# Where the next unit's first retention job stands: a slot inside the last job of the present unit

## The chip, the cores and the metric

The kernel runs on one core of one Trainium2 chip. The metric is the device time of one execution in microseconds (us). Engines are named as in the profile: PE is TensorE's matmul and PEld its weight load, DVE is VectorE, ACT is ScalarE, POOL is GpSimd, SP is SyncE, which here only issues DMAs.

## The reference

All numbers are float32. Retention in its parallel form runs over 8 batches, 8 heads, 576 positions and 64 dimensions a head; its output, reshaped to 4608 tokens of 512, goes through an RMS norm and a SwiGLU network of width 1536.

```python
# q, k, v: (8, 8, 576, 64)
scores = (1.0 / np.sqrt(D_)) * np.matmul(q, k.transpose(0, 1, 3, 2))
gamma = 1.0 - 2.0 ** (-5.0 - np.arange(H))
rel = pos[:, None] - pos[None, :]
Dmat = np.where(rel >= 0, gamma[:, None, None] ** rel[None, :, :], 0.0)
attn = np.matmul(scores * Dmat[None], v)
x = attn.transpose(0, 2, 1, 3).reshape(B * S, H * D)          # (4608, 512)
xn = x / np.sqrt(np.mean(x * x, axis=-1, keepdims=True) + 1e-06) * rms_g
g = xn @ w_gate
out = (g / (1.0 + np.exp(-g)) * (xn @ w_val)) @ w_out
```

## The kernel before

**Retention jobs.** A job is one batch and one pair of heads; there are 32 (8 batches, 4 pairs), `jobs[j]`. The sequence of a job is cut into nine chunks of 64 positions, so all its matmuls are 64x64 and run on quarters of the PE array, one head of the pair beside the other. A job has these parts:

- `fetch(j)`: SP issues the DMAs of q, k and v (L160, L201, L204).
- `prepare(j)`: DVE transposes q and k (two instructions, L257), ACT scales v by the decay (four, L266).
- `scores(j)` (L285): q times k within each chunk, 40 matmuls in the trace. A float32 matmul stands there as two matmuls with two weight loads.
- `states(j)` (L305): k times v of each chunk, 32 in the trace.
- `weigh(j)`: DVE masks the scores (two instructions, L318) into `ret`.
- `sums(j)`: DVE sums the states up over the chunks with the decay (eight instructions, L332 and L334).
- `values(j)` (L355): masked scores times v into two PSUM banks, 36 in the trace. At its end ACT copies one element into `tick` (`valued`, L364), waiting for the last matmul.
- `carried(j)` (L375): q times the running sums, added into the same banks, 32 in the trace; its first matmul waits for `valued`. Then DVE writes four to six scaled pieces into x (L397).

`slot(j, rest)` puts two jobs together: `values(j - 1)`, `scores(j)`, `states(j)`, `weigh(j)`, `carried(j - 1)`, and then `sums(j)`. Without `rest` it has only job j's parts. `close(j)` is `values(j)` and `carried(j)`.

**Units.** The feed-forward network runs over nine units of 512 tokens. Units 0 and 1, with jobs 0 to 11, stand in a written plan (`PLAN`), which the change doesn't touch. Units 2 to 8 run in the loop at the end of the kernel. A unit has six steps `up(u, n)` for the first two weight matrices and then `across(u)` for the third. Both use a scheme that multiplies two-by-two blocks with seven products instead of eight. `up` is a generator: it gives way seven times, i = 0 to 6, once after each of its seven products; a product is four matmuls of 128x256, eight in the trace (L614), and the names x, y, z, x, w, z, w of the banks are their order. Odd n multiply into `h` on DVE (L621, L633) and take differences (`differences`, L698); even n apply SiLU on ACT (L635).

**What is put between.** The order on every engine is the order in which these calls are made (`tc.manual_schedule`); nothing is moved by a scheduler. In units 2 to 6 (`more`) the retention jobs of one batch stand between the steps of `up`: unit u takes jobs j0 = 4(u + 1) to j0 + 3. After n = 0 comes `slot(j0)` without the rest, after n = 1, 2 and 3 a full `slot(j0 + n)`; `values(j0 + 3)` stands before the last product of n = 4 (i = 5), and `carried(j0 + 3)` after n = 4. These are six stretches of 64x64 matmuls. `prepare(j0 + n)` and `fetch(j0 + n + 1)` stand in n = 1 to 4 at i = 2, so the next unit's first job is prepared in n = 4. In n = 5 ACT squares the four columns of the next unit's x, DVE adds them up (`gather`, L446 and L440), and after i = 4 `root_1` sums them over partitions with one 128x512 matmul (L477).

**Buffers.** PSUM has eight banks, taken in turn by `bank()`: four by a step of `up`, two by `values`, four by `scores` and `states`. q and k transposed and the running sums have two buffers each, `ret` one, v three and k four. Weights come through a ring in SBUF, which `refill` (L580) fills when `used` frees a piece.

Of the kernel before, what the change touches and what calls it, by code (L numbers as in the profile page):

```python
# [41 lines left out]
def kernel(  # L42
# [15 lines left out]
    NHP = H // 2  # L58
# [87 lines left out]
    jobs = [(b, hp) for b in range(B) for hp in range(NHP)]  # L146
# [125 lines left out]
    def side(i):  # L272
        return slice(i * L, i * L + L)
# [3 lines left out]
    def scores(j):  # L277

        d = st[j]
        s = d["s"] = [bank(f"s_{j}_{i}") for i in range(3)]  # L280
        for c in range(NC + 1):
            i, odd = divmod(c, 2)
            c = min(c, NC - 1)
            for e in range(2):
                nc.tensor.matmul(  # L285
                    s[e][side(odd), i * L : i * L + L], lhsT=d["kT"][side(e), c * L : c * L + L],
                    rhs=d["qT"][side(e), c * L : c * L + L], start=True, stop=True,
                )
# [8 lines left out]
    def states(j):  # L297

        d = st[j]
        d["last"] = bank(f"last_{j}")  # L300
        for c in range(NC - 1):
            i, odd = divmod(c, 2)
            o = state_of(d, c)
            for e in range(2):
                nc.tensor.matmul(  # L305
                    o[side(e)], lhsT=d["k"][side(odd), i, e],
                    rhs=d["v"][side(odd), i, e], start=True, stop=True,
                )

    def weigh(j):  # L310

        d = st[j]
        hp = jobs[j][1]
        s = d["s"]
        n = NFULL + 1
        ret = d["ret"] = att.tile([P, 2, n, L], F32, tag="ret", name=f"ret_{j}", bufs=1)
        for e in range(2):
            nc.vector.scalar_tensor_tensor(  # L318
                out=ret[:, e], in0=s[e][:, : n * L].rearrange("p (c k) -> p c k", k=L),
                scalar=float(_gamma(H)[2 * hp + e] ** -L),  # L320
                in1=causal.unsqueeze(1).to_broadcast([P, n, L]), op0=ALU.mult, op1=ALU.mult,
            )

    def sums(j):

        d = st[j]
        hp = jobs[j][1]
        t = d["sum"] = att.tile([P, NC - 1, L], F32, tag="sum", name=f"sum_{j}")
        for c in range(NC - 1):
            part = state_of(d, c)  # L330
            if c == 0:
                nc.vector.tensor_copy(out=t[:, 0], in_=part)  # L332
                continue
            nc.vector.scalar_tensor_tensor(  # L334
                out=t[:, c], in0=t[:, c - 1], scalar=gc[:, hp : hp + 1], in1=part,
                op0=ALU.mult, op1=ALU.add,
            )
        del d["s"], d["last"]

    def follow(a, b):  # L340
        why = mybir.DependencyInfo(mybir.DependencyClass.Sync, mybir.DependencyReason.DATA)
        tc.add_manual_dep(a.ins, b.ins.name, why, reason="rows of the array")

    def column(j, odd, e):

        return side(1 - e if odd and j >= FIRST else e)

    def values(j):

        d = st[j]  # L350
        av = d["av"] = [bank(f"av_{j}_{i}") for i in range(2)]
        for c in range(NC):
            i, odd = divmod(c, 2)
            for e in range(2):
                mm = nc.tensor.matmul(  # L355
                    av[odd][column(j, odd, e), i * L : i * L + L],
                    lhsT=d["v"][side(odd), i, e] if c < NC - 1 else d["vt"][:, e],
                    rhs=d["ret"][side(odd), e, i],
                    start=(c < 2), stop=False, skip_group_check=True,
                )  # L360
        if j < FIRST:
            d["valued"] = nc.gpsimd.memset(tick, 0.0)
        else:
            d["valued"] = nc.scalar.copy(out=tick, in_=mhalf[:1])  # L364
        follow(d["valued"], mm)

    def carried(j):

        d = st[j]
        b, hp = jobs[j]  # L370
        av = d["av"]
        for c in range(1, NC):
            i, odd = divmod(c, 2)
            for e in range(2):
                mm = nc.tensor.matmul(  # L375
                    av[odd][column(j, odd, e), i * L : i * L + L], lhsT=d["sum"][side(e), c - 1],
                    rhs=d["qT"][side(e), c * L : c * L + L],
                    start=False, stop=(c >= NC - 2), skip_group_check=True,
                )
                if c == 1 and e == 0:  # L380
                    follow(mm, d["valued"])
        cut = U // L - b
        for u, c0, c1, o in ((b, 0, cut, b * L), (b + 1, cut, NC, 0)):
            if u not in x_of:
                x_of[u] = xp.tile([P, NHP, U], F32, tag="x", name=f"x_{u}")
            x = x_of[u][:, hp, o : o + (c1 - c0) * L].rearrange("p (c k) -> p c k", k=L)
            for first in (c0, c0 + 1):
                i, odd = divmod(first, 2)
                n = -(-(c1 - first) // 2)
                if n <= 0:  # L390
                    continue
                moves = [(slice(0, P),) * 2]
                if column(j, odd, 0) != side(0):
                    moves = [(side(e), column(j, odd, e)) for e in range(2)]
                for to, at in moves:
                    g = (gq if to == at else gx)[at, hp].unsqueeze(1)
                    nc.vector.tensor_tensor(  # L397
                        out=x[to, first - c0 :: 2],
                        in0=av[odd][at, i * L : (i + n) * L].rearrange("p (c k) -> p c k", k=L),
                        in1=g.to_broadcast([at.stop - at.start, n, L]), op=ALU.mult,  # L400
                    )
        st[j] = {}

    def slot(j, rest=True):

        if rest:
            values(j - 1)
        scores(j)
        states(j)
        weigh(j)  # L410
        if j < FIRST:
            sums(j)
        if rest:
            carried(j - 1)
        if j >= FIRST:
            sums(j)
# [5 lines left out]
    def fetch(j):  # L422
        if j < len(jobs):
            load_qk(j)
            load_kv(j)
# [557 lines left out]
    def store(u, b=None):  # L983

        rows = out[u * U : u * U + U].rearrange("(C c p) (R r x) -> c r p C R x", C=2, c=2, R=2, r=2)
        v4 = vec.rearrange("p (C R) n d -> p C R n d", C=2)
        for n, (r, c) in CORNERS.items():
            if b is None:
                for half in range(2):
                    nc.sync.dma_start(out=rows[c][r][:, half], in_=v4[:, half, :, n])  # L990
            else:
                nc.sync.dma_start(out=rows[c][r][:, b // 2, b % 2], in_=vec[:, b, n])
# [246 lines left out]
    with tc.manual_schedule():  # L1239
        start()  # L1240
        for u in range(2, NU):
            j0 = NHP * (u + 1)
            more = u + 1 < B
            for n in range(2 * NG):
                for i, _ in enumerate(up(u, n)):
                    if n == 1 and i == 4:
                        store(u - 1)
                    if n == 2 * NG - 2 and i == 1:
                        inner_sums(u, 0, 0)
                        inner_sums(u, 1, 0)  # L1250
                    if more and i == 2 and 0 < n <= NHP:
                        if j0 + n < len(jobs):
                            prepare(j0 + n)
                            fetch(j0 + n + 1)
                    if u + 1 < NU and n == 2 * NG - 1:
                        if i < NHP:
                            gather(u + 1, i, square(u + 1, i))
                        elif i == NHP:
                            root_1(u + 1)
                    if more and n == NHP and i == 5:  # L1260
                        values(j0 + NHP - 1)
                if more and n < NHP:
                    slot(j0 + n, rest=(n > 0))
                elif more and n == NHP:
                    carried(j0 + NHP - 1)
            for i, _ in enumerate(across(u)):
                if u + 1 == NU:
                    continue
                if i == 2:
                    root_2(u + 1)  # L1270
                elif i in (3, 4, 5, 6):
                    scale_x(u + 1, (i - 3,))
                elif i == 8:
                    sums_of_x(u + 1)
# [27 lines left out]
```

## Time and profile before

| | us |
|---|---|
| median of 3 runs | 1116.55 (1115.22 to 1117.88) |
| the profiled execution, its own time | 1118.5 |
| its span, first to last instruction | 1116.6 |
| PE busy in the span | 1093.8 |
| DVE busy | 798.5 |
| POOL busy | 467.8 |
| ACT busy | 279.9 |
| 64x64 matmuls of scores, busy (L285) | 28.2 |
| 64x64 matmuls of the carried part, busy (L375) | 27.2 |

The mean granted TensorE clock of the profiled execution was 0.994. A line of the timeline gives the start and the duration in us, the engine, the line of the code, the operation, what it writes and reads, the tile of the array (128\*128 is the whole, 64\*64 a quarter), the size and the number of instructions that are merged into the line. Idle time before it stands in brackets with what ended it; "issue" is time in which the engine waited for nothing that the profile shows. Matmuls are pipelined, so the durations of merged lines overlap, and only starts can be subtracted from each other.

### The profile page before, as it was taken

To read this page: it belongs to the slowest core of one execution; us is meant where nothing else is said; L and a number is where in the kernel's file an instruction comes from. 1 tells how busy PE (TensorE), PEld (TensorE's weight loads), DVE (VectorE), ACT (ScalarE), POOL (GpSimd) and SP (SyncE) were. 2 spreads that over 40 slices of the span, in tenths; PEclk is the share of its full clock that TensorE was granted. 3 is DMA by queue.
4 is the path that set the end of the run, shared out by engine and by line. 5 is a ranking of instruction groups with operands and counts; after the bars stand their busy time and mean duration, and the time that the engine had idled before them with its cause. 6 is when DMAs were issued, how large, how long until landed. Compare 5 with 4: busy or idle time off the path is not lost.

```text
span 1116.6 us, 24381 instructions
## 1 busy us (share of the span) xinstructions
PE 1093.8 (98%) x10102; PEld 915.3 (82%) x10102; DVE 798.5 (72%) x1367; ACT 279.9 (25%) x565; POOL 467.8 (42%) x419
## 2 busy tenths in 40 slices
PE   7899999999999999999999999999999999999998
PEld 6754444469988899889988898889888998898888
DVE  3777768789867786787677786779476945594456
ACT  4556465211121221222022201231122111211110
POOL 0023535557730287025802482229312951393236
PEclk8899999999999999999999999999999999999999
DMA  7765888598678976787769875898485665585471
GB/s 178 205 183 190 285 228 241 211 318 238 221 306 211 207 251 220 212 226 218 281 162 212 284 254 160 242 234 289 150 216 199 238 213 181 165 293 166 158 243 42
DMA packets 253870, 243.72 MB, mean 218 GB/s; under 512 B 193088, under 2 KB 213824, under 8 KB 247616
## 3 DMA queue, kind: packets, MB, share of 16 engines
q1 hardware_dynamic: 252752, 241.87, 70.8%
q8 instruction: 79, 1.29, 0.5%
q10 hardware_dynamic: 1008, 0.30, 0.1%
q14 instruction: 31, 0.25, 0.1%
HBM read 212.05 MB, written 30.08 MB: 217 GB/s over the span
## 4 chain that ended last, share of the span: by engine, by line
PE 90%; DVE 6%; issue 1%; POOL 1%; ACT 1%; DMA 0%; SPq 0%; POOLq 0%; DVEq 0%; ACTq 0%
PE up L674 14%; PE x L614 13%; PE z L614 13%; PE w L614 13%; PE y L614 7%; PE xo L773 6%; PE xp L773 4%; PE zo L773 3%; PE zp L773 3%; PE yo L773 2%; PE av L355 2%; PE wo L773 2%; PE s L285 2%; PE av L375 2%; PE yp L773 1%
## 5 line engine op out<-in xcount | busy, mean ns | idle before, releaser
L674 PE MATMUL up<-x,ring 128*128 128x512 f32 x384 | 166.9, 594 | 1.3 <-DVE x L521 0.8
L614 PE MATMUL x<-x,ring 128*128 128x256 f32 x672 | 161.4, 383 | 0.6 <-DVE t L698 0.6
L738 POOL TENSOR_TENSOR vi<-h 128x384 f32<-128x384 f32 x32 | 38.9, 1217 | 288.6 <-DVE h L633 273.3
L614 PE MATMUL w<-sums,ring 128*128 128x256 f32 x672 | 159.3, 380 | 0.0
L614 PE MATMUL z<-x,ring 128*128 128x256 f32 x672 | 158.7, 379 | 0.0
L674 PEld LDWEIGHTS up<-x,ring 128*128 128x128 f32 x384 | 72.3, 190 | 90.6 <-issue 83.9
L614 PEld LDWEIGHTS z<-x,ring 128*128 128x128 f32 x672 | 127.7, 190 | 19.9 <-issue 2.9
L614 PEld LDWEIGHTS w<-sums,ring 128*128 128x128 f32 x672 | 127.3, 190 | 17.4
L614 PEld LDWEIGHTS x<-x,ring 128*128 128x128 f32 x672 | 125.1, 190 | 18.1 <-DVE t L698 0.7
L743 POOL TENSOR_TENSOR vi<-h 128x384 f32<-128x384 f32 (+2 forms) x46 | 48.0, 1042 | 147.0 <-DVE h L633 147.0
L977 POOL TENSOR_TENSOR vi<-vi 128x512 f32<-128x512 f32 (+2 forms) x63 | 71.9, 1153 | 35.4 <-DVE vi L800 32.6
L640 ACT COPY m<-x 128x512 f32<-128x512 f32 x42 | 24.6, 585 | 229.3 <-PE x L614 229.3
L614 PE MATMUL y<-sums,ring 128*128 128x256 f32 x336 | 79.4, 379 | 0.9 <-DVE sums L533 0.9
L621 DVE TENSOR_TENSOR h<-u,w 128x512 f32<-128x512 f32 x42 | 28.9, 687 | 62.7 <-PE w L614 62.4
L614 PEld LDWEIGHTS y<-sums,ring 128*128 128x128 f32 x336 | 63.8, 190 | 9.9 <-PE x L614 1.3
L621 DVE TENSOR_TENSOR u<-m,y 128x512 f32<-128x512 f32 x42 | 28.8, 685 | 48.1 <-PE y L614 45.4
L635 ACT ACTIVATE h<-h 128x512 f32<-128x512 f32 x63 | 39.6, 630 | 85.3 <-DVE h L621 85.3
L334 DVE SCALAR_TENSOR_TENSOR sum<-sum,gc,s 128x64 f32<-128x64 f32 x192 | 53.9, 281 | 6.8
L1097 POOL TENSOR_TENSOR vi<-vi 128x512 f32<-128x512 f32 (+1 forms) x24 | 40.7, 1698 | 40.7 <-DVE vi L1086 26.8
L743 POOL TENSOR_TENSOR vi<-vi,h 128x384 f32<-128x384 f32 (+2 forms) x46 | 48.9, 1062 | 3.6
L743 POOL TENSOR_TENSOR vi<-h,vi 128x384 f32<-128x384 f32 (+2 forms) x46 | 46.2, 1005 | 3.6
L1097 POOL TENSOR_TENSOR ring<-ring 128x512 f32<-128x512 f32 x24 | 30.4, 1272 | 41.1 <-DVE ring L1086 30.7
(310 smaller groups left out, 2050.1 us busy)
## 6 DMA issues: line engine op xcount, KB each, us to landing
ring<-w_out_blocks SPq DMA_DIRECT2D x59, 1344.0 KB, 6.6
ring<-w_up_blocks SPq DMA_DIRECT2D x42, 1792.0 KB, 8.0
w_out_blocks<-vi SPq DMA_DIRECT2D x21, 448.0 KB, 4.4
out_dram<-vi SPq DMA_DIRECT2D x64, 128.0 KB, 3.1
qraw<-in_q_dram SPq DMA_DIRECT2D x96, 72.0 KB, 5.2
kraw<-in_k_dram SPq DMA_DIRECT2D x96, 72.0 KB, 3.2
k<-in_k_dram SPq DMA_DIRECT2D x48, 128.0 KB, 3.1
v<-in_v_dram SPq DMA_DIRECT2D x48, 128.0 KB, 3.0
```

The costliest lines, as they stand in the source:

```text
L285: nc.tensor.matmul(s[e][side(odd), i * L : i * L + L], lhsT=d["kT"][side(e), c * L : c * L + L], rhs=d["qT"][side(e), c * L : c * L + L], ...
L334: nc.vector.scalar_tensor_tensor(out=t[:, c], in0=t[:, c - 1], scalar=gc[:, hp : hp + 1], in1=part, op0=ALU.mult, op1=ALU.add,)
L614: nc.tensor.matmul(ps[:, i * HU : i * HU + HU], lhsT=w[:, PLACE[blk], c, i * P : i * P + P], rhs=t_of[u][blk][:, c], start=(start and i == ...
L621: nc.vector.tensor_tensor(out=o, in0=a, in1=pairs_of(ps), op=ALU.add)
L635: nc.scalar.activation(out=o, in_=c, func=AF.Silu)
L640: nc.scalar.copy(out=s1, in_=pairs_of(x_))
L674: nc.tensor.matmul(ps, lhsT=w[:, PLACE[blk], c % 2, i * P : i * P + P], rhs=x_of[u][:, c], start=(c == 0), stop=(c == NHP - 1),)
L738: eng.tensor_tensor(out=i1, in0=x12, in1=x11, op=ALU.subtract)
L743: eng.tensor_tensor(out=o[:, c], in0=a[:, c], in1=b[:, c], op=op)
L773: nc.tensor.matmul(ps, lhsT=lhs[:, c], rhs=w[:, s, c], start=((nm, s // 4) not in first), stop=False, skip_group_check=True,)
L977: eng.tensor_tensor(out=t[:, :, o], in0=t[:, :, x], in1=t[:, :, y], op=ALU.add)
L1097: nc.gpsimd.tensor_tensor(out=t[o], in0=t[x], in1=t[y], op=op)
```

## The change

The loop of the units gets another condition. After n = 4, too, a full slot is put: `slot(j0 + 4)`, which is `values(j0 + 3)`, scores and states of the next unit's first job, its `weigh`, `carried(j0 + 3)` and its `sums`. Since that job is then done with its first half, no slot stands after n = 0, except in unit 2, whose first job no unit ahead of it took. In unit 6, where there is no next job, `values` stays before the last product of n = 4 and `carried` after the step. The lines that prepare and fetch stay as they are.

```diff
-                    if more and n == NHP and i == 5:
+                    if more and (n, i) == (NHP, 5) and j0 + NHP == len(jobs):
                         values(j0 + NHP - 1)
-                if more and n < NHP:
-                    slot(j0 + n, rest=(n > 0))
-                elif more and n == NHP:
-                    carried(j0 + NHP - 1)
+                if more and n <= NHP and (n or u == 2):
+                    if j0 + n < len(jobs):
+                        slot(j0 + n, rest=(n > 0))
+                    else:
+                        carried(j0 + n - 1)
```

In the built programs each engine has the same instructions of computation and DMA in both; on PE, DVE and ACT some change places, on POOL and SP none does. PE's program has 44 stretches of 64x64 matmuls before and 36 after, the written plan's among them.

## The prediction

> **What bounds the kernel now.** I read the page first: the busy line and the chain that ended last.
>
> ```profile
> span 1116.6 us, 24381 instructions
> PE 1093.8 (98%) x10102; PEld 915.3 (82%) x10102; DVE 798.5 (72%) x1367; ACT 279.9 (25%) x565; POOL 467.8 (42%) x419
> ...
> q8 instruction: 79, 1.29, 0.5%
> ...
> PE 90%; DVE 6%; issue 1%; POOL 1%; ACT 1%; DMA 0%; SPq 0%; POOLq 0%; DVEq 0%; ACTq 0%
> ```
>
> TensorE (PE) is busy for 98% of the span and carries 90% of the chain. From 300 us on, the PE timeline has only four marked pauses (0.91, 1.17, 0.61 and 0.72 us). So in the units the change touches, the end moves by what PE's own queue gains or loses. DVE, ACT, POOL and SP count only if they make PE wait.
>
> "Busy" hides what the change is about, so next I read the PE timeline of unit 5 by start times, not by durations (ends are modelled). A step of one `product` is eight 128x256 matmuls, and start to start it takes 1.727 us. Here are the first stretch (after n=0), the full slot after n=3, and the two pieces of n=4:
>
> ```profile
> 677.28 1.89 PE L614 MATMUL w<-sums,ring 128*128 128x256 f32 x8
> 679.10 0.81 PE L285 MATMUL s<-qT,kT 64*64 64x64 f32 x40
> ...
> 680.31 1.99 PE L614 MATMUL x<-x,ring 128*128 128x256 f32 x8
> 682.14 1.89 PE L614 MATMUL y<-sums,ring 128*128 128x256 f32 x8
> ...
> 719.87 1.89 PE L614 MATMUL w<-sums,ring 128*128 128x256 f32 x8
> 721.69 0.69 PE L355 MATMUL av<-ret,v 64*64 64x64 f32 x32
> ...
> 723.37 0.67 PE L375 MATMUL av<-qT,sum 64*64 64x64 f32 x32
> 723.97 1.99 PE L614 MATMUL x<-x,ring 128*128 128x256 f32 x8
> 725.80 1.89 PE L614 MATMUL y<-sums,ring 128*128 128x256 f32 x8
> ...
> 732.71 1.89 PE L614 MATMUL z<-x,ring 128*128 128x256 f32 x8
> 734.53 0.69 PE L355 MATMUL av<-ret,v 64*64 64x64 f32 x32
> 735.04 0.28 PE L355 MATMUL av<-ret,vt 64*64 64x64 f32 x4
> 735.26 1.99 PE L614 MATMUL w<-sums,ring 128*128 128x256 f32 x8
> 737.18 0.69 PE L375 MATMUL av<-qT,sum 64*64 64x64 f32 x32
> 737.81 1.99 PE L614 MATMUL x<-x,ring 128*128 128x256 f32 x8
> 739.64 1.89 PE L614 MATMUL y<-sums,ring 128*128 128x256 f32 x8
> ```
>
> The reader is to see that the step ahead of a stretch takes 1.82 us until the stretch starts (721.69 - 719.87), not 1.727, and the step behind it 1.83 (725.80 - 723.97): both edges of every stretch cost time, however short it is.
>
> **What the Trainium skill says.** "TensorEngine Tiling (Array Packing)", section Key Properties: changing the tiling mode, not just the tile, drains TensorE. The trace agrees as far as it goes: about 0.1 us at each visible edge. "Runtime: NRT & Kernel Launch", section Instruction fetch mechanics: an engine's instructions arrive in blocks of 16 KiB (256 instructions) that it fetches itself over a DMA queue. The trace agrees on the size: q8 moved 1.29 MB in 79 packets, 16.3 KB each. The page calls a block's crossing mostly hidden; the trace shows where it may not be:
>
> ```profile
> 356.43 0.55 PE L375 MATMUL av<-qT,sum 64*64 64x64 f32 x24
> 358.16 0.34 PE L375 MATMUL av<-qT,sum 64*64 64x64 f32 x8 [1.17 <-issue]
> ```
>
> PE stops in the middle of a run of matmuls with nothing to wait for. I counted TensorE's instructions in the built program (an f32 matmul is two loads and two matmuls in the trace). This stop and the 0.61 us one at 490.44 stand a whole multiple of 256 apart (11 blocks), and each ends a block that lay wholly in a full slot (281 instructions in 2.3 us). That is my inference for both.
>
> **The change part by part, cost by cost.**
>
> *Removed and added on PE.* Each stretch's cost is the time from the last 128-wide step's start ahead of it to the second one's start behind it, less 1.727 per step between. Unit 5: n=0: 682.14 - 677.28 - 2 x 1.727 = 1.41. Full slot n=3: 725.80 - 719.87 - 3.454 = 2.48. n=4, both pieces: 739.64 - 732.71 - 3 x 1.727 = 1.75. The same subtraction in units 2 to 6 gives 1.40 to 1.41 for n=0 and 1.75 for n=4 each time; the fifteen full slots give 2.44 to 2.49, save the two with the pauses above (3.88 and 3.16). A join takes away one n=0 stretch and one split n=4 and puts one full slot in their place: 1.41 + 1.75 - 2.48 = 0.68 us. As a check, 72 matmuls at 1.41 and 140 at 2.48 give 0.016 us a matmul and a fixed 0.28 a stretch; two stretches fewer are 0.56, and the split n=4 is 0.12 dearer than that line.
>
> *How often.* The joins lie between units 2 and 3, 3 and 4, 4 and 5, 5 and 6. Unit 2 keeps its n=0 slot and unit 6 its split close, as there is no job 32. The built program has 36 stretches, not 44: eight fewer, four joins. 4 x 0.68 = **2.7 us off the path**.
>
> *Moved on DVE.* Two masks (L318) and eight running sums (L332, L334) of the next unit's first job, some 3.2 us, move from n=1's begin to n=5's begin. There they stand ahead of n=5's adds and of the squares' sums, which end in the matmul of `root_1` (L477). Cover: DVE idles there today (1.82 us before n=5's first add, then 0.37 and 0.44). The last links now:
>
> ```profile
> 745.02 0.69 DVE L633 TENSOR_TENSOR h<-h,x 128x512 f32<-128x512 f32 x1 [0.44 <-PE x L614]
> 745.62 0.68 DVE L440 SCALAR_TENSOR_TENSOR sq<-sq,sq 128x512 f32<-128x512 f32 x1
> ```
>
> The L477 matmul starts at 746.54, 0.24 after L440 ends. With T the start of n=5 on PE (737.81), L633 starts at T + 7.21. Slot n=2 is the model for the new n=4 (even n, no `differences`): its first add behind the sums starts 4.3 to 4.6 us after its T (713.80 - 709.40; 596.95 - 592.64; 479.82 - 475.20). From there n=5 queues add, square sum, add, square sum, 2.6 us by their starts: free at T + 6.9 to T + 7.2, in time for T + 7.21. I take 0. If it slips, PE waits at L477 for the slip: from 0 up to 0.5 us a join, 2 us in all.
>
> *Moved on ACT and the wait for it.* `valued` (L364) now stands behind the last SiLU of n=4 (L635), not ahead of it, and the first `carried` matmul waits for it; behind that on PE is all of n=5. In slot n=2 the order is the same: that copy starts at 708.49, lasts 0.17, and `carried` starts at 708.80. All n=2 slots without a pause cost 2.48, as n=3's do. I take 0; the scores and states between hide it.
>
> *Earlier need of loads.* Job j0+4's k, v and transposes were needed a whole `across` later; now at n=4's end. SP's order and the prepare and fetch steps do not move, nor does a DMA pass another. In unit 5 the scaled v is ready at 734.4 and the new states would start near 737.5; margins in units 2 to 4 are 5.5 us or more. Buffers of k, v, qT, sum and the ring are freed no later. The slot takes four more PSUM banks before n=5, as at n=1 to 3, whose next products don't wait. I take 0; a load later by more than 3 us would cost the excess.
>
> *Instruction blocks.* Counting on from the two pauses, the new slots begin 13 instructions after a block's edge (unit 2) and have the next edge 142, 42 and 197 instructions in (units 3, 4, 5). No block lies wholly in one of them. Edge to edge the tightest takes about 3.5 us (unit 2), against 3.3 and 2.7 us at the two pauses, in which the block was late. I take 0; from -0.6 (the pause in unit 3 may go) to 1.4 a slot (the dearer pause: 3.88 - 2.48).
>
> **Sum.** -2.7 us. The profiled execution took 1118.5 us (span 1116.6 and 1.9 around it): it would become 1115.8. The median of the runs is 1116.55, so 1113.9 there (-0.24%).
>
> **The rivals.**
> 1. *Joined as above, no new wait:* 1113.9. For it: fifteen slots of this very form in this trace. Against it: the gain is as small as the spread of the three runs (1115.22 to 1117.88).
> 2. *A wait takes back part.* DVE's queue makes L477 late in four units by up to 0.5, or one fetch pause of 1.2 to 1.4 comes: -2.7 + 1.4 = -1.3, 1115.2. For: only 0.24 us of slack at L477, 2 of 15 full slots pause. Against: the add chain catches up by L633; no block fits.
> 3. *Slower: instruction fetch.* If my block count is off, each of the four longer bursts can empty the fetched instructions. Place: the end of each new slot; price 1.4 each: 4 x 1.4 - 2.7 = +2.9, 1119.4. It decides from two such pauses on. For: only full slots pause here, none of the ten short pieces. Against: thirteen of fifteen don't.
> 4. *It does nothing:* the edges cost the same inside a slot, where values, scores and carried parts follow each other. Then 1116.5. Against: the slot's 2.48 is measured with those inside.
>
> **Chances.** Rival 1 0.68, 2 0.17, 3 0.09, 4 0.06. A difference of about 0.2% (2.2 us) is what a measurement of this kernel can tell from no change, and -2.7 is close to it: of case 1, 0.61 falls beyond it and 0.07 within. Faster 0.61, within 0.30, slower 0.09. The range: up to 1116.0 takes in case 2; down to 1112.2 is the forecast less the -0.6 of a lost pause and 1.1 of spread of the runs.
>
> **What would show it.** Right: in units 2 to 5 after n=4 one stretch L355, L285, L305, L375 of 2.48 by the same subtraction, and n=0 running into n=1 at 1.727 a step; L477 without an idle mark; PE busy time some 2 to 3 us less. Wrong: an idle mark on L477 from DVE, on L375 from ACT or "issue" in the new slots, or on L305 from a load.

## The result and the profile after

The changed kernel took 1113.79 us in the median of 13 runs (1112.17 to 1118.05), the kernel before 1116.55 (13 runs, 1114.98 to 1118.05). The ratio is 0.9979, 95% interval 0.997 to 0.9988: 0.21% faster, 2.3 us by the ratio and 2.8 by the medians. Forecast were 1113.9 and 2.7 less. The interval stands for a gain of some 1.3 to 3.3 us, so it holds gains of under 0.2% as well as of over, and that the median came within 0.1 us of the forecast is closer than these runs can tell.

The page of the changed kernel, the lines that answer to those shown of before:

```profile
span 1113.8 us, 24383 instructions
PE 1092.8 (98%) x10102; PEld 916.3 (82%) x10102; DVE 798.5 (72%) x1367; ACT 279.6 (25%) x565; POOL 467.6 (42%) x419
...
q8 instruction: 79, 1.29, 0.5%
...
PE 90%; DVE 5%; SPq 2%; issue 1%; POOL 1%; ACT 1%; DMA 0%; POOLq 0%; DVEq 0%; ACTq 0%
```

The page tells next to nothing of the change: the same number of matmuls, PE at 98%, and 1.0 us less busy time. The change has to be read in PE's timeline. In unit 5 of the changed kernel, the new slot behind n=4:

```profile
732.29 1.89 PE L614 MATMUL w<-sums,ring 128*128 128x256 f32 x8
734.11 0.70 PE L355 MATMUL av<-ret,v 64*64 64x64 f32 x32
...
735.79 0.67 PE L375 MATMUL av<-qT,sum 64*64 64x64 f32 x32
736.39 1.99 PE L614 MATMUL x<-x,ring 128*128 128x256 f32 x8
738.23 1.89 PE L614 MATMUL y<-sums,ring 128*128 128x256 f32 x8
```

By the prediction's subtraction it costs 738.23 - 732.29 - 3.454 = 2.49 us. In units 2 to 5 the new slots cost 2.51, 2.49, 2.49 and 2.49. And n=0 now runs into n=1 with plain steps of 1.73:

```profile
676.54 1.89 PE L614 MATMUL w<-sums,ring 128*128 128x256 f32 x8
678.27 1.89 PE L614 MATMUL x<-x,ring 128*128 128x256 f32 x8
680.00 1.89 PE L614 MATMUL y<-sums,ring 128*128 128x256 f32 x8
```

**Why the two profiled executions can't just be subtracted.** Their spans differ by 2.8 us, as forecast, but partly by luck. The same marked line, the y product of unit 2's n=0, starts at 316.20 before and at 313.95 after: 2.25 us come from units 0 and 1, which the change doesn't touch. Here is that line and the last marked pause, before and then after:

```profile
316.20 1.97 PE L614 MATMUL y<-sums,ring 128*128 128x256 f32 x8 [0.91 <-DVE sums L533]
...
1084.75 1.60 PE L773 MATMUL xo<-ring,h 128*128 128x128 f32 x12 [0.72 <-ACT vi L788]
```

```profile
313.95 1.97 PE L614 MATMUL y<-sums,ring 128*128 128x256 f32 x8 [0.91 <-DVE sums L533]
...
1081.93 1.60 PE L773 MATMUL xo<-ring,h 128*128 128x128 f32 x12 [0.72 <-ACT vi L788]
```

Then the slot of unit 2's n=2, also untouched, loses more than before:

```profile
356.73 0.34 PE L375 MATMUL av<-qT,sum 64*64 64x64 f32 x8 [1.99 <-issue]
357.00 2.67 PE L614 MATMUL x<-x,ring 128*128 128x256 f32 x8
359.47 2.94 PE L614 MATMUL y<-sums,ring 128*128 128x256 f32 x8
```

The pause is 1.99 us, not 1.17, and the two products behind it take 2.47 and 2.78 us instead of 1.83 and 1.73. So I compare a part of the execution that contains all the change: from that y product of unit 2 to the end of the last marked pause, in front of xo. It takes 768.55 us before and 767.98 after. From this I take what the pauses that the prediction put down to instruction fetch ("fetch pauses" from here on) cost beyond a slot without one: before 3.88 - 2.48 and 3.16 - 2.48, 2.08 in all; after 5.34 - 2.48 for the slot up to the y product, 1.05 for that product, and 0.28 in unit 3's n=3 slot, 4.19 in all. What remains is 766.47 and 763.79: **2.68 us less**. The result doesn't hang on this correction: in the second profile of the changed kernel the pauses cost about what they do before, and its part is 2.88 us shorter as it stands. The same for every kernel below is in this table.

| kernel | stretches in units 2 to 6 | part | fetch pauses in it | part without them | against before | ratio of the times, 95% |
|---|---|---|---|---|---|---|
| before | 30 | 768.55 | 2.08 | 766.47 | | |
| changed | 22 | 767.98 | 4.19 | 763.79 | -2.68 | 0.9979 (0.997 to 0.9988) |
| changed, run again | 22 | 765.67 | 1.92 | 763.75 | -2.72 | 0.9979 (0.9971 to 0.9987) |
| e1, half the join | 26 | 767.43 | 2.38 | 765.05 | -1.42 | 0.9988 (0.9981 to 0.9996) |
| e2, moved, not joined | 30 | 768.72 | 2.26 | 766.46 | -0.01 | 1.0005 (0.9997 to 1.0013) |
| e3, all slots split | 41 | 771.08 | 0.58 | 770.50 | +4.03 | 1.0022 (1.0015 to 1.003) |
| e6, 52 instructions ahead | 22 | 766.58 | 2.73 | 763.85 | -2.62 | 1.003 (1.0018 to 1.0042) |
| e7, blocks set | 22 | 764.45 | 0 | 764.45 | -2.02 | 0.9971 (0.9959 to 0.9983) |

### The profile page after: what moved, and what is told of

It is laid out like the page before. It is cut to its first block, busy times and chain, and to the rows that moved or that the text cites. A ratio compares the mean times of both kernels' runs of the same rounds, so it can differ in the third digit from the quotient of the medians.

```text
span 1113.8 us, 24383 instructions
## 1 busy us (share of the span) xinstructions
PE 1092.8 (98%) x10102; PEld 916.3 (82%) x10102; DVE 798.5 (72%) x1367; ACT 279.6 (25%) x565; POOL 467.6 (42%) x419
## 4 chain that ended last, share of the span: by engine, by line
PE 90%; DVE 5%; SPq 2%; issue 1%; POOL 1%; ACT 1%; DMA 0%; POOLq 0%; DVEq 0%; ACTq 0%
PE up L674 14%; PE x L614 13%; PE w L614 13%; PE z L614 13%; PE y L614 7%; PE xo L773 6%; PE xp L773 4%; PE zo L773 3%; PE zp L773 3%; PE yo L773 2%; PE wo L773 2%; PE av L355 2%; PE s L285 2%; PE av L375 2%; PE yp L773 1%
## 5 line engine op out<-in xcount | busy, mean ns | idle before, releaser
L640 ACT COPY m<-x 128x512 f32<-128x512 f32 x42 | 24.6, 585 | 231.1 <-PE x L614 231.1
```

What stands on the lines that cost most here:

```text
L640: nc.scalar.copy(out=s1, in_=pairs_of(x_))
```

## The experiments

The theory: every stretch of 64x64 matmuls between 128-wide ones has a fixed price, whatever lies in it, and the change saves eight of them. The first rival: the gain comes from the work that left n=0 and n=1. The second: the edges cost the same inside a slot, where values, scores and carried parts follow each other. The edits are shown against the changed kernel.

**e1: half the join.**

```diff
-                    if more and (n, i) == (NHP, 5) and j0 + NHP == len(jobs):
+                    if more and (n, i) == (NHP, 5):
                         values(j0 + NHP - 1)
...
-                if more and n <= NHP and (n or u == 2):
-                    if j0 + n < len(jobs):
-                        slot(j0 + n, rest=(n > 0))
-                    else:
-                        carried(j0 + n - 1)
+                if more and n < NHP and (n or u == 2):
+                    slot(j0 + n, rest=(n > 0))
+                elif more and n == NHP:
+                    carried(j0 + n - 1)
+                    if j0 + n < len(jobs):
+                        slot(j0 + n, rest=False)
```

> Values(j0+3) stays before the last product of n=4; behind n=4 come carried(j0+3) and then, in the same stretch, scores and states of the next unit's first job. The program has 40 stretches (44 before, 36 after), and DVE's masks and sums stand at n=5's begin as in the changed kernel. Theory (each stretch has a fixed price of about 0.3 us, whatever lies in it): the two pieces cost 1.02 + (0.28 + 104 x 0.0157) = 2.9 us by starts, against 3.16 before and 2.49 after, so about 0.9 us less than before, some 1115.6. Rival (the gain comes from work that left n=0 and n=1, on DVE too): as the changed kernel, 2.7 less than before.

Measured: ratio 0.9988, some 1.3 us less than before; in the part without pauses 1.42 less, half of the changed kernel's 2.68, for half of its stretches. DVE has its masks and sums where the changed kernel has them, so the first rival falls. The expected 0.9 was too small because it added the prices of two stretches that share one step, and so counted the 0.2 us that this step is longer than 1.727 twice. The right way round, from the z product to the y product, it is 738.05 - 730.08 - 3 x 1.727 = 2.79, 0.37 less than 3.16.

**e2: the same work moved, nothing joined.**

```diff
-                    if j0 + n < len(jobs):
-                        slot(j0 + n, rest=(n > 0))
-                    else:
-                        carried(j0 + n - 1)
+                elif more and n == NHP:
+                    carried(j0 + n - 1)
+                elif more and n == NHP + 1 and j0 + NHP < len(jobs):
+                    slot(j0 + NHP, rest=False)
```

(The condition on `values` and the slots of n < 4 are as in e1.)

> Close of the last job as before (values, then carried behind n=4), and the next unit's first job as a stretch of its own behind n=5 instead of behind the next unit's n=0. 44 stretches as before; n=0 and n=1 of units 3 to 6 are as free as in the changed kernel. Theory: the stretches cost 1.41 and 1.75 as before, no gain, within 0.5 us of before. Rival (relief of n=0 and n=1): 2.7 us less than before, as the changed kernel.

Measured: 1.0005, and -0.01 us in the part. Units 3 to 6 have n=0 and n=1 as free as in the changed kernel, and nothing is gained. It is the number of stretches that counts, not their place.

**e3: the other way, every slot split.**

```diff
-                    if more and (n, i) == (NHP, 5) and j0 + NHP == len(jobs):
-                        values(j0 + NHP - 1)
+                    if more and n and n <= NHP and i == 5:
+                        values(j0 + n - 1)
...
-                        slot(j0 + n, rest=(n > 0))
+                        slot(j0 + n, rest=(n > 0), early=(n > 0))
```

With `early`, `slot` leaves `values` out.

> The changed kernel with values(j - 1) put before the last product of n=1 to 4 in every unit, and the rest of the slot behind the step: 55 stretches, 19 more than the changed kernel. Theory: each split costs 0.45 us by starts (1.02 + 1.91 - 2.48), 8.5 us in all, less 1 to 3 us of fetch pauses in units 2 and 3, since no block of 256 instructions fits into the halves: 5.5 to 7.5 us over the changed kernel. Rival (the edges cost the same inside a slot, where values, scores and carried follow each other): no more than the changed kernel.

Unit 5's n=4 in this kernel, which is now split as in the kernel before, but with scores and states in its second half:

```profile
734.09 1.89 PE L614 MATMUL z<-x,ring 128*128 128x256 f32 x8
735.91 0.69 PE L355 MATMUL av<-ret,v 64*64 64x64 f32 x32
...
736.64 1.99 PE L614 MATMUL w<-sums,ring 128*128 128x256 f32 x8
738.56 0.81 PE L285 MATMUL s<-qT,kT 64*64 64x64 f32 x40
...
740.26 1.99 PE L614 MATMUL x<-x,ring 128*128 128x256 f32 x8
742.09 1.89 PE L614 MATMUL y<-sums,ring 128*128 128x256 f32 x8
```

742.09 - 734.09 - 3 x 1.727 = 2.82, 0.34 more than a whole slot. Measured in all: 1.0022 against the 0.9979 of the changed kernel, 0.43% or 4.8 us; in the part, 6.7 us over the changed kernel for 19 more stretches, 0.35 each. The times fall short of the expected 5.5 to 7.5 because its 0.45 for a split counts the shared step's 0.2 us twice, too. The second rival falls: the edges inside a slot are not like those to 128-wide matmuls.

**e4 and e5: the price by itself.** In units 7 and 8, which have no retention work, needless matmuls stand ahead of each step: in e4 on a 64x64 quarter, in e5 on the whole array (128 in the place of each `:64` of rows and weights).

```diff
         x_, y, z, w_ = (bank(f"{nm}_{u}_{n}") for nm in "xyzw")
+        if u > NU - 3:
+            for _ in range(1 if u == NU - 2 else 18):
+                nc.tensor.matmul(
+                    x_[:64, :64], lhsT=w[:64, PLACE[A11], 0, :64], rhs=t_of[u][A11][:64, 0, :64],
+                    start=True, stop=False, skip_group_check=True,
+                )
```

> The changed kernel with needless 64x64x64 matmuls ahead of each step's first product in units 7 and 8, which have no retention work: one in each of unit 7's six steps (2 in the trace), 18 in each of unit 8's (36 in the trace). What they write is overwritten. They all use one quarter of the array. Theory of the fixed price: about 0.3 us for the step edge with one, so the price is there with hardly any work in the stretch; with 18 it is that plus the work. Rival (the price is that of the retention work itself, its waits and its rows): one matmul costs 0.03 us.

> The same places and counts with 128x128 weights and 64 columns, so that the array's tile never changes. Theory of the fixed price of changing the tile: one costs only its two passes of 64 columns, 0.1 to 0.15 us by starts, and no fixed price beyond; 18 cost 36 such passes, about 2 to 2.5 us. Rival (any short matmul between the steps costs an edge): about 0.3 us as with the 64x64 ones, and more with 18.

One needless matmul in unit 7, first of e4, then of e5 (its two passes are the line L640):

```profile
910.63 1.89 PE L614 MATMUL w<-sums,ring 128*128 128x256 f32 x8
912.45 0.33 PE L640 MATMUL x<-x,ring 64*64 64x64 f32 x2
912.71 1.99 PE L614 MATMUL x<-x,ring 128*128 128x256 f32 x8
914.54 1.89 PE L614 MATMUL y<-sums,ring 128*128 128x256 f32 x8
```

```profile
910.41 1.89 PE L614 MATMUL w<-sums,ring 128*128 128x256 f32 x8
912.14 0.33 PE L640 MATMUL x<-x,ring 128*128 128x64 f32 x2
912.31 1.95 PE L614 MATMUL x<-x,ring 128*128 128x256 f32 x8
914.09 1.89 PE L614 MATMUL y<-sums,ring 128*128 128x256 f32 x8
```

In e4 one costs 914.54 - 910.63 - 3.454 = 0.46 us, in e5 0.23. In unit 8, where 18 stand in the same place, e4 and e5 have

```profile
1021.54 1.89 PE L614 MATMUL w<-sums,ring 128*128 128x256 f32 x8
...
1027.43 1.89 PE L614 MATMUL y<-sums,ring 128*128 128x256 f32 x8
```

```profile
1021.76 1.89 PE L614 MATMUL w<-sums,ring 128*128 128x256 f32 x8
...
1029.23 1.89 PE L614 MATMUL y<-sums,ring 128*128 128x256 f32 x8
```

so 36 passes cost 1027.43 - 1021.54 - 3.454 = 2.44 and 1029.23 - 1021.76 - 3.454 = 4.02. A pass costs (2.44 - 0.46) / 34 = 0.058 us in one quarter and (4.016 - 0.226) / 34 = 0.1115 on the whole array, and what is left of the single matmul is 0.46 - 2 x 0.058 = **0.34 us with a change of the tile** and 0.226 - 2 x 0.1115 = **0.00 without**. That is the price in question, free of all retention work, and it equals the 0.34 per stretch of the change. (The whole kernels took 1135.1 and 1143.27 us in one execution each, against 1116.61 of the kernel before.) My sizes for e5 were too small: a pass of 64 columns with 128x128 weights takes as long as one of 128 columns (0.112 in `across`, where 12 take 1.34).

**e6: 52 instructions ahead of everything.** This tests the prediction's reading of the pauses, that a block of 256 instructions which lies wholly in a full slot comes late.

```diff
             for e in range(2):
-                nc.tensor.matmul(
+                for _ in range(14 if j == 0 and c == e == 0 else 1):
+                  nc.tensor.matmul(
                     s[e][side(odd), i * L : i * L + L], lhsT=d["kT"][side(e), c * L : c * L + L],
                     rhs=d["qT"][side(e), c * L : c * L + L], start=True, stop=True,
-                )
+                  )
```

> The changed kernel with the first scores matmul of job 0 repeated 13 times (it writes the same values again): 52 more instructions on TensorE ahead of everything, 0.4 us of work. Theory of the pauses (an instruction block of 256 that lies wholly in a full slot is late): the pauses in unit 2's n=2 slot, in unit 3's n=3 slot and at the end of the carried part at about 36 to 40 us go; if one comes, it is in unit 4's n=2 slot. 2 to 5 us less than the changed kernel. Rival (the pauses belong to the DMA traffic at those places, not to the count of instructions): they stay where they are, and the time is that of the changed kernel plus 0.4.

Units 2 and 3 have no pause now: their slots cost 2.45 to 2.52, all of them. The pauses have moved to unit 4's n=2 slot, which was named, and to unit 5's n=3 slot, which was not: there the next edge comes just behind the slot's 282 instructions, in the first product. Unit 4's:

```profile
592.51 0.57 PE L376 MATMUL av<-qT,sum 64*64 64x64 f32 x25
594.51 0.34 PE L376 MATMUL av<-qT,sum 64*64 64x64 f32 x7 [1.42 <-issue]
```

The time was expected to fall and rose: 1.003 (1.0018 to 1.0042). In the part from unit 2 on the kernel is as fast as the changed one. It loses before that: its y product of unit 2 starts at 320.07, against 313.95, 6.12 later. The first scores, with the repeats, take 3.74 us (11.08 to 14.82, where the states start) against 0.63 (10.48 to 11.11). So the 26 repeated passes cost 3.1 us, where I had put 0.4; that is 0.12 a pass, twice e4's 0.058, and the trace doesn't show why. The other 3.0 us are lost by the first feed-forward matmul of unit 0 (64.72 against 58.59); behind it the two profiles keep their distance within 0.01 us up to unit 2. Ahead of it PE waits for issue in four places, 4.8 us in all, against two and 3.5; the pause that was to go from the carried part is 1.49 us at 35.07, in place of 1.83 at 35.94. What else adds to the 3.0 is open.

**e7: the blocks set.** Nine products of `up` are issued as halves, 16 more instructions each, so that no block lies in a full slot from unit 2 on, and nothing changes ahead of unit 2.

```diff
+    HALVED = {(2, 2): 3, (3, 0): 1, (4, 1): 1, (5, 0): 3, (6, 1): 1}
...
         def product(blk, ps, start):
+            halves_ = blk in (A11, S2, S1)[: HALVED.get((u, n), 0)]
+            cut = HU // 2 if halves_ else HU
             for i in range(2):
                 for c in range(2):
-                    nc.tensor.matmul(
-                        ps[:, i * HU : i * HU + HU], lhsT=w[:, PLACE[blk], c, i * P : i * P + P],
-                        rhs=t_of[u][blk][:, c], start=(start and i == c == 0), stop=False,
-                        skip_group_check=True,
-                    )
+                    for k in range(0, HU, cut):
+                        nc.tensor.matmul(
+                            ps[:, i * HU + k : i * HU + k + cut],
+                            lhsT=w[:, PLACE[blk], c, i * P : i * P + P],
+                            rhs=t_of[u][blk][:, c, k : k + cut],
+                            start=(start and i == c == k == 0), stop=False,
+                            skip_group_check=True,
+                        )
```

> The changed kernel with nine of the up products of units 2 to 6 issued as halves (eight 128x128 matmuls in place of four 128x256): 16 more instructions each on TensorE, put where they move the edges of the instruction blocks so that no block of 256 lies in a full slot from unit 2 on; all the rest is as in the changed kernel. The halves cost about 0.06 us a product, 0.5 in all. Theory of the blocks: no pause marked issue in any slot of units 2 to 6, every full slot 2.44 to 2.52 us by starts; the changed kernel's pauses there (2.9 + 0.3 us in its profile) go, 1 to 3 us less than the changed kernel. Rival (the pauses come from the DMA traffic at those places): pauses stay in units 2 and 3, 0.5 us more than the changed kernel.

> The changed kernel as it is, beside the one with the blocks set, on the same chip: 2.7 us less than before by the price of eight stretches, with pauses in unit 2's n=2 slot and unit 3's n=3 slot again, if they belong to the count of instructions.

The changed kernel, run again, has its two pauses in the same two slots (3.82 and 3.06 us). With the blocks set there is none. Unit 2's n=2 slot:

```profile
350.53 1.89 PE L619 MATMUL w<-sums,ring 128*128 128x256 f32 x8
...
354.63 2.00 PE L619 MATMUL x<-x,ring 128*128 128x256 f32 x8
356.46 1.89 PE L619 MATMUL y<-sums,ring 128*128 128x256 f32 x8
```

Every full slot of units 2 to 6 costs 2.44 to 2.54, and between the two marked lines that begin and end the part PE has no marked pause at all. The halves cost 0.66 us (764.45 against 763.79). So 1.2 us of the 1.92 are left as a gain in the part. In the times it is 0.9971 (0.9959 to 0.9983) against 0.9979 (0.9971 to 0.9987) on the same chip: medians of 1113.93 and 1114.83, with intervals that overlap. It is the fastest version I have, and clearly faster than before, but not shown to be faster than the changed kernel, let alone by the 1 to 3 us expected.

**What all the pauses share.** The traces say more than e6 and e7 were made for. If PE's matmuls, weight loads and sequencer instructions are counted in their order, every pause of PE marked "issue", in all ten profiles, stands a whole multiple of 256 from every other, and PE goes on 1.3 to 1.6 us after a packet of q8 has ended (for the first of the kernel before, 358.16 and 356.70). The 0.61 us pause of unit 3 belongs to them, though the profile puts it down to DVE:

```profile
490.44 1.99 PE L614 MATMUL x<-x,ring 128*128 128x256 f32 x8 [0.61 <-DVE t L698]
```

Its packet ended at 489.04. So the count says where PE can run dry, but not whether it does. Unit 6's n=1 slot holds a whole block in both kernels (edges 9 and 265 instructions in before, 3 and 259 after) and costs 2.44 without a pause; and e3 has a pause of 0.43 us (at 624.51) behind a block that took 5.5 us. In the kernel before, the mean busy share of the DMA engines was 0.66 around that slot of unit 6 (804 to 812) and 0.91 and 0.92 around its two pauses (350 to 358, 483 to 490). That such traffic makes a block late fits, but no run here varies it alone.

## Why the prediction was right

- **PE sets the end.** Held: the part without pauses moved by what PE's stretches moved, in all eight profiles.
- **1.41 + 1.75 - 2.48 = 0.68 a join, four joins.** Held: the new slots cost 2.49 to 2.51, and 2.68 us went, against 2.7. With 22 stretches in place of 30 that is 0.34 a stretch, as e1 (0.35), e3 (0.37) and e4 (0.34) have it.
- **The edges cost, not the work.** Held: e4 has the price with one matmul in the stretch, e5 has none without the change of the tile. That it is the drain which the Trainium skill names in "TensorEngine Tiling (Array Packing)", section Key Properties, fits, but these runs show only that it comes with the tile. The prediction's 0.28 from two points was low by 0.06, and the 0.12 by which it found the split n=4 dearer is this 0.06 twice, for its two stretches.
- **DVE's moved work is hidden.** Held. DVE of the changed kernel in unit 5, T = 736.39:

```profile
740.79 0.68 DVE L621 TENSOR_TENSOR u<-m,y 128x512 f32<-128x512 f32 x1
...
743.61 0.69 DVE L633 TENSOR_TENSOR h<-h,x 128x512 f32<-128x512 f32 x1 [0.34 <-PE x L614]
744.21 0.69 DVE L440 SCALAR_TENSOR_TENSOR sq<-sq,sq 128x512 f32<-128x512 f32 x1
```

The first add comes at T + 4.40 (expected 4.3 to 4.6), DVE waits for PE again at L633 (T + 7.22), and L477 on PE starts at 745.13, 0.23 after L440's end, as before.
- **ACT's copy and the loads are in time.** Held: the copy ends at 735.65 and `carried` starts at 735.79; v is ready at 732.77 and the states start at 735.32, 2.6 us later.
- **No instruction block in a new slot.** Held: the new slots have no marked pause, and e6 and e7 show that the count, not the place in the code, decides where pauses can stand. "Runtime: NRT & Kernel Launch", section Instruction fetch mechanics, has the 256 instructions right for this case and calls the crossing mostly hidden; so it is here, but not always in a run of small matmuls: from unit 2 on it cost 2.08 us in the profile before, 4.19 and 1.92 in those of the changed kernel. That scatter is as large as the gain, and that it did not hide the gain in the times is the work of many executions.
- **What was wrong.** PE's busy time was to fall by 2 to 3 us and fell by 1.0 on the page, and by 4.0 (to 1089.8) on that of the second profile. In the part alone it falls from 766.05 to 765.20 and to 763.47; in the first of these the two slow products behind the long pause count as busy, 0.64 and 1.05 us more than usual, and without them both have some 2.5 less. The pause in unit 3, which "may go", was smaller (0.28 and 0.58 against 0.68), not gone. And the prediction's reading of the pauses was too strict: that a block lies wholly in a full slot is neither enough (unit 6's n=1 slot, in its own trace) nor needed (e3).

## What to carry to other kernels

Short runs of quarter-array matmuls between full-array ones are worth joining: each had a fixed price, 0.34 us here. The profile marks no idle time for it and counts it as busy, so it is read by subtracting the starts of the neighbours. Before a run is made longer, count its instructions: one that went through a whole fetch block in some 2 us could run PE dry. And where single executions scatter by more than the change is worth, compare the part that holds the change, with the pauses taken out.

## What was not expected of the hardware

- **Behind a pause of 2 us the clock was lower.** In the stretch of time behind the 1.99 us pause of the changed kernel the granted clock was 0.65; behind the 1.17 us pause of the kernel before it was 1.00. The columns are the length, each engine's busy time with its count, the clock, DMA share and GB/s:

```profile
357.00:361.00 4.00, 4.00 (x19) 3.33 (x13) 3.53 (x13) 0.59 (x1) 0.00 (x0) 0.65 0.61 101
```

```profile
358.00:362.00 4.00, 3.84 (x25) 3.36 (x26) 3.14 (x12) 0.58 (x1) 0.00 (x0) 1.00 0.88 116
```

  In e5 the pause in the same slot was 1.75 us, and from 360 to 364 the clock was 1.00. So the longest pause, with the slow products, cost 3.9 us where the one before cost 1.4. It is one case of each: that the length of the pause is the cause fits, but is not shown.
- **The scatter of the runs has a place.** Among the profiles of kernels that are alike up to unit 2 (before, changed twice, e1, e2, e3, e4, e5, e7), the y product of unit 2 starts between 313.62 and 317.89 us. From there on, without the pauses, two profiles of the changed kernel agree within 0.04 us. Nearly all of that scatter stands ahead of the first feed-forward matmul of unit 0, which starts between 58.15 and 62.53; from there to the y product the nine take 255.35 to 255.6. PE's waits for issue ahead of it sum to between 2.5 and 6.3 us; what else varies there is open.
